# First loads of a fused attention and feed-forward kernel: 2 KB query runs, two heads on a partition, and gate weights loaded by row halves

## The chip, the cores and the metric

One core of a Trainium2 chip. The metric is the device time of one execution in microseconds (us). "us" of a timed run and "span" of its profile are not the same thing: the span leaves out about 2 us at the edges. A "run" of 1 KB or 2 KB is a contiguous stretch of memory that a load reads; it shows in the DMA views as one packet. A run is called slow when it lies over 1.5% above the fastest of its kernel.

## The reference

Linear attention without softmax, an RMS norm per head, then an RMS norm over all heads and a gated feed-forward network:

```python
kv  = einsum("bhsd,bhse->bhde", k, v)            # q, k, v: 8 x 8 x 576 x 64, fp32
out = einsum("bhsd,bhde->bhse", q, kv)
out = out / sqrt(mean(out*out, -1) + 1e-6) * g_norm
x   = out.transpose(0, 2, 1, 3).reshape(8*576, 512)
xn  = x / sqrt(mean(x*x, -1) + 1e-6) * rms_g
y   = (silu(xn @ w_gate) * (xn @ w_val)) @ w_out   # d_ff = 1536
```

## The kernel before: the parts that matter

The work goes batch by batch. PE (the matmul engine) is fed from weights that are loaded as fp32, scaled by `rms_g` and rounded to bf16 on POOL, DVE and ACT (`round_w`), and from queries that are cast to bf16 and transposed on PE. All loads below are issued by SP (`nc.sync`), but for the first value loads and two tiny gain loads by ACT (`nc.scalar`).

Loads of the first batch and of the first weights (`S` = 576, `H` = 8 heads, `NS` = 4 row groups of the weights; cuts are marked):

```python
    q0 = stage().rearrange("p (f h x) -> p f h x", f=2, h=H // 2)

    def load_q0(f, queue):                        # token half f, 256 tokens
        dst = q0[:, f].rearrange("(p g) h x -> p g h x", g=2)
        for g in range(2):                        # 4 tokens of a head are one run: 1 KB
            src = q[0, 4 * g : 4 * g + 4, 256 * f : 256 * f + 256, :].rearrange("h (p t) d -> p h (t d)", t=4)
            queue.dma_start(out=dst[:, g], in_=src)

    for j in (0, 1):
        load_kv(0, "k", nc.sync, slice(j, j + 1))
        load_kv(0, "v", nc.scalar, slice(j, j + 1))
    ...                                           # two loads of gains into gam on nc.scalar
    load_q0(0, nc.sync)
    for j in (2, 3):
        load_kv(0, "k", nc.sync, slice(j, j + 1))
        load_kv(0, "v", nc.sync, slice(j, j + 1))
    load_q0(1, nc.sync)
    load_w("g", (0, 1), False)                    # block 0, then block 1: 1 KB runs
    load_w("v", (0, 1), True)                     # rows 0, 1 of both blocks, then 2, 3: 2 KB runs
```

The order of work on the first weights. `round_w(block, name, row group, engine)` makes one block of 256 columns of one row group ready; `GP` is POOL, `SC` is ACT:

```python
    for s in range(NS):
        round_w(0, "g", s, GP)
    for s in (0, 1):
        round_w(1, "g", s, GP)
    ...
    round_w(1, "g", 2, DVE)
    round_w(1, "g", 3, SC)
    for blk, s in ((0, 0), (0, 1), (1, 0), (1, 1), (0, 2), (1, 2)):
        round_w(blk, "v", s, GP)
    ...                                           # PE: gate products of block 0 in between them
    Z.sums()                                      # the norm's sums of the second token half
    ...
```

After these come the next loads, in this order, and some 20 us later the transposes of the second batch's queries on PE, between parts of the first batch's last product.

```python
    ...                                           # the other gate and value blocks
    load_kv(1, "k", nc.sync)
    load_wo(0, (0,))
    load_kv(1, "v", nc.sync)
    load_wo(0, (2,))                              # second half of a block of the last weights
    load_q(1)                                     # second batch's queries, two loads of 4 heads
    ...
    for c in range(4):
        down_part(c, 0, 2)
    ...                                           # second batch: kv products; casts of its queries
    down_part(0, 2, 4)                            # needs the second half of that block
    turns.q_turn(0, SC)                           # PE transposes; needs both loads of load_q(1)
    down_part(1, 2, 4)
    turns.q_turn(1, DVE)
```

Of the kernel before, what the change touches and what calls it, by code (L numbers as in the profile page):

```python
# [11 lines left out]
BF16 = mybir.dt.bfloat16  # L12
# [8 lines left out]
def kernel(  # L21
# [12 lines left out]
    nc = tc.nc  # L34

    B, H, S, D = q.shape
# [8 lines left out]
    NS = d_model // 128  # L45
# [30 lines left out]
    PE, DVE, SC, GP = nc.tensor, nc.vector, nc.scalar, nc.gpsimd  # L76

    identity = consts.tile([128, 128], BF16, name="identity")
# [20 lines left out]
    def stage(n=2048):  # L99
        return stage_pool.tile([128, NS * C * D], FP32, name="st")[:, 0:n]  # L100

    def cast(engine, dst, src):
        if engine is SC:
            engine.copy(out=dst, in_=src)  # L104
        else:
            engine.tensor_copy(out=dst, in_=src)  # L106
# [7 lines left out]
    def alloc_kv(b, name):  # L114
        raws[b, name] = stage(NS * C * D).rearrange("p (j x) -> p j x", j=NS)
# [51 lines left out]
    def load_w(name, blks, split):  # L167

        widths = [(W_BLOCKS[b][1] - W_BLOCKS[b][0]) * 128 for b in blks]
        j0 = W_BLOCKS[blks[0]][0] * 128  # L170
        view, flat, at = {"g": wg_view, "v": wv_view}[name], stage(), 0
        whole = flat[:, 0 : NS * sum(widths)].rearrange("p (s f) -> p s f", s=NS)
        for b, w in zip(blks, widths):
            if split:
                w_st[name, b] = whole[:, :, at : at + w]
            else:
                w_st[name, b] = flat[:, NS * at : NS * (at + w)].rearrange("p (s f) -> p s f", s=NS)
                nc.sync.dma_start(out=w_st[name, b], in_=view[:, :, j0 + at : j0 + at + w])
            at += w
        if split:  # L180
            for s in (0, 2):
                nc.sync.dma_start(out=whole[:, s : s + 2], in_=view[:, s : s + 2, j0 : j0 + at])
# [282 lines left out]
    class Ffn:  # L465
# [68 lines left out]
        def down_out(self, c, engine=None):  # L534
            if c % 2 == 0:
                self.o_sb = osb_pool.tile([128, 2, d_model], FP32, name="o_sb")
            cast(engine or SC, self.o_sb[:, c % 2, :], self.o_ps[c])
            n = self.n
            if n == B:
                for u in range(2):  # L540
                    r0 = (2 * c + u) * S + MAIN
                    nc.sync.dma_start(
                        out=out[r0 : r0 + TAIL, :], in_=self.o_sb[u * TAIL : (u + 1) * TAIL, c % 2, :]
                    )
            elif c % 2 == 1 and n == 0:
                r0 = 256 * (c // 2)
                rows = out[r0 : r0 + 256, :].rearrange("(p c t) d -> t p c d", c=2, t=2)
                for t in range(2):
                    nc.sync.dma_start(out=rows[t], in_=self.o_sb[64 * t : 64 * t + 64])
            elif c % 2 == 1:  # L550
                rows = out[n * S : n * S + MAIN, :].rearrange("(p t) d -> p t d", t=T)[:, c - 1 : c + 1, :]
                nc.sync.dma_start(out=rows, in_=self.o_sb)
# [32 lines left out]
    b0 = 0  # L585
    for name in ("k", "v"):
        alloc_kv(0, name)
    q0 = stage().rearrange("p (f h x) -> p f h x", f=2, h=H // 2)

    def load_q0(f, queue):  # L590

        dst = q0[:, f].rearrange("(p g) h x -> p g h x", g=2)
        for g in range(2):
            src = q[0, 4 * g : 4 * g + 4, 256 * f : 256 * f + 256, :].rearrange("h (p t) d -> p h (t d)", t=4)
            queue.dma_start(out=dst[:, g], in_=src)

    for j in (0, 1):
        load_kv(0, "k", nc.sync, slice(j, j + 1))
# [4 lines left out]
        out=gam[NS : NS + 1, :].rearrange("o (i d) -> o i d", i=2),  # L603
        in_=g_norm.rearrange("(o d) -> o d", o=1).unsqueeze(1).to_broadcast([1, 2, D]),
    )
    load_q0(0, nc.sync)
    for j in (2, 3):
        load_kv(0, "k", nc.sync, slice(j, j + 1))
        load_kv(0, "v", nc.sync, slice(j, j + 1))
    load_q0(1, nc.sync)  # L610
    load_w("g", (0, 1), False)
    load_w("v", (0, 1), True)

    make_identity(nc, identity)
    make_identity(nc, ident32)
# [11 lines left out]
    def warm(ps, count, w=512):  # L627
        for _ in range(count):
            PE.matmul(ps[:, 0:w], lhsT=warm_sb[:, 0:128], rhs=warm_sb[:, 0:w], start=True, stop=True, skip_group_check=True)  # L629
# [5 lines left out]
    qb0 = bufs[0]["q"]  # L635
    qt0 = qt_pool.tile([128, NS, MAIN], BF16, name="qt")
# [1 line left out]
    A = Cols(0, 0, 256, qt0, sqt0, "A")  # L638
    Z = Cols(0, 256, 512, qt0, sqt0, "Z")

    qb0 = qb0.rearrange("p t h d -> p (t h d)").rearrange("p (f t h d) -> p f t h d", f=2, t=4, h=4)

    def cast_q0(f, hs, engine):
        cast(engine, qb0[:, f, :, hs, :], q0[:, f, hs, :].rearrange("p h (t d) -> p t h d", t=4))

    def turn_q0(f, dummies):
        bank = att_pool.tile([128, 512], FP32, name="att_ps")
        warm(bank, dummies)
        ps = bank.bitcast(BF16).rearrange("p (j t x) -> p j t x", j=2, t=4)
        for j in range(2):  # L650
            for t in range(4):
                PE.matmul(
                    ps[:, j, t, :], lhsT=qb0[:, f, t, 2 * j : 2 * j + 2, :], rhs=identity,
                    is_transpose=True, start=(j == 0 and t == 0), stop=(j == 1 and t == 3),
                )
        return ps.rearrange("p j t (x g) -> p j t x g", g=2)

    def put_q0(f, ps, g, engine):
        dst = qt0[:, 2 * g : 2 * g + 2, 256 * f : 256 * f + 256].rearrange("p j (t x) -> p j t x", t=4)
        cast(engine, dst, ps[:, :, :, :, g])  # L660

    def state0(j, dummies):
        ps = att_pool.tile([128, 512], FP32, name="att_ps")
# [30 lines left out]
            cols.o_products(c, banks[c])  # L694
        return banks

    hs0, hs1 = slice(0, 2), slice(2, 4)

    warm_ps = att_pool.tile([128, 512], FP32, name="att_ps")
    warm(warm_ps, 9)  # L700
# [1 line left out]
    for j in (0, 1):  # L702
# [3 lines left out]
    kv1 = state0(1, 3)  # L706
    put_state0(0, kv0)
    cast_q0(0, hs0, DVE)
    cast_q0(0, hs1, SC)
    put_state0(1, kv1)  # L710
    banksA = [gps_pool.tile([128, MAIN], FP32, name="g_ps"), vps_pool.tile([128, MAIN], FP32, name="v_ps")]
    qps = turn_q0(0, 2)
    cast_kv(0, "k", 2, DVE)
    cast_kv(0, "v", 2, SC)
    put_q0(0, qps, 0, DVE)
    put_q0(0, qps, 1, SC)
    kv2 = state0(2, 3)
    cast_kv(0, "k", 3, DVE)
# [13 lines left out]
        out=gsq, in0=gcol, scalar=1.0 / d_model, in1=gcol, op0=OP.mult, op1=OP.mult  # L732
# [9 lines left out]
    A.sums()  # L742
    oA = rows_of(A)
    cast_q0(1, hs0, SC)
    cast_q0(1, hs1, GP)
    A.head()
    A.root_by_table(lambda: None)
    banksZ = [gps_pool.tile([128, MAIN], FP32, name="g_ps"), vps_pool.tile([128, MAIN], FP32, name="v_ps")]
    qps = turn_q0(1, 2)
    warm(banksZ[0], 2)  # L750
    for g in range(2):
        put_q0(1, qps, g, SC)
# [321 lines left out]
```

## Time and profile before

| what | value |
|---|---|
| time, three runs | 319.03 median (318.98 to 319.62) us |
| time, six runs beside the changed kernel (the three are among them) | 319.4 median, 319.45 mean (318.98 to 319.96) us |
| span of the profile, granted clock | 317.6 us, 0.998 |
| PE busy | 97% of the span |
| start of PE's row of 16 gate and value products (the head's weights are there) | 22.43 us |
| cast of the second half of batch 1's queries | 42.51 us |
| start of batch 1's first attention products on PE | 45.48 us |

The last three are the marks by which I compare profiles.

Third, the timeline at 42 to 44 us. DVE, idle, waits 0.81 us for a load of batch 1's queries (in brackets), casts it, and the eight transposes on PE, which take 0.61 us where nothing holds them, take 0.99.

```profile
42.51 0.63 DVE L106 CAST qb<-st 128x512 bf16<-128x512 f32 x2 [0.81 <-DMA st<-in_q_dram]
42.73 0.99 PE L843 MATMUL g_ps<-identity,qb 128*128 128x128 bf16 x8
43.78 0.38 PE L529 MATMUL o_ps<-wo_sb,h_sb 128*128 128x512 bf16 x1
```

### The profile page before, as it was taken

To read this page: it belongs to the slowest core of one execution; us is meant where nothing else is said; L and a number is where in the kernel's file an instruction comes from. 1 tells how busy PE (TensorE), PEld (TensorE's weight loads), DVE (VectorE), ACT (ScalarE), POOL (GpSimd) and SP (SyncE) were. 2 spreads that over 40 slices of the span, in tenths; PEclk is the share of its full clock that TensorE was granted. 3 is DMA by queue.
4 is the path that set the end of the run, shared out by engine and by line. 5 is a ranking of instruction groups with operands and counts; after the bars stand their busy time and mean duration, and the time that the engine had idled before them with its cause. 6 is when DMAs were issued, how large, how long until landed. Compare 5 with 4: busy or idle time off the path is not lost.

```text
span 317.6 us, 5996 instructions
## 1 busy us (share of the span) xinstructions
PE 308.5 (97%) x2334; PEld 150.3 (47%) x2371; DVE 181.3 (57%) x378; ACT 175.6 (55%) x323; POOL 21.5 (7%) x46
## 2 busy tenths in 40 slices
PE   7899999999999999999999999999999999999995
PEld 3575446444444444444444444444444444444443
DVE  3776768679339922893289327941795079504310
ACT  3577367485667465746683768376745374233321
POOL 1174351100000000000000000000000000000000
PEclk9999999999999999999999999999999999999999
DMA  7999999685369267904790489939002710230014
GB/s 266 358 385 388 375 375 333 145 275 215 90 180 344 86 138 187 369 9 108 189 378 22 98 172 207 354 66 181 22 0 60 140 66 3 57 141 3 0 33 100
DMA packets 60712, 54.95 MB, mean 173 GB/s; under 512 B 36232, under 2 KB 45708, under 8 KB 60684
## 3 DMA queue, kind: packets, MB, share of 16 engines
q1 hardware_dynamic: 60304, 53.92, 56.7%
q10 hardware_dynamic: 380, 0.66, 0.6%
q8 instruction: 18, 0.29, 0.4%
q14 instruction: 10, 0.08, 0.1%
HBM read 37.75 MB, written 9.44 MB: 149 GB/s over the span
## 4 chain that ended last, share of the span: by engine, by line
PE 90%; DMA 5%; SPq 1%; another core or an unknown queue 1%; issue 1%; POOL 1%; DVE 0%; ACT 0%
PE v_ps L477 28%; PE g_ps L477 28%; PE o_ps L529 26%; DMA st<-in_moe_w_val_dram 3%; DMA st<-in_q_dram 2%; PE att_ps L286 2%; PE v_ps L529 1%; PE g_ps L529 1%; DMA out_dram<-o_sb 1%; PE att_ps L326 1%; PE o_ps L494 1%; POOL wv_sb L191 1%; PE o_ps L326 0%; PE att_ps L262 0%
## 5 line engine op out<-in xcount | busy, mean ns | idle before, releaser
L483 DVE TENSOR_TENSOR h_sb<-silu,v_ps 128x512 bf16<-128x512 bf16 x104 | 71.1, 684 | 99.9 <-ACT silu L482 68.1
L477 PE MATMUL v_ps<-xnt,wv_sb 128*128 128x512 bf16 x409 | 106.2, 379 | 0.7
L477 PE MATMUL g_ps<-xnt,wg_sb 128*128 128x512 bf16 x398 | 104.6, 379 | 0.7
L482 ACT ACTIVATE silu<-g_ps 128x512 bf16<-128x512 f32 x104 | 62.1, 597 | 70.1 <-PE g_ps L477 58.4
L529 PE MATMUL o_ps<-wo_sb,h_sb 128*128 128x512 bf16 x386 | 86.8, 379 | 0.4
L477 PEld LDWEIGHTS <-wv_sb 128*128 128x128 bf16 x416 | 40.7, 98 | 49.1
L529 PEld LDWEIGHTS <-h_sb 128*128 128x128 bf16 x420 | 40.6, 98 | 47.6 <-issue 0.4
L477 PEld LDWEIGHTS <-wg_sb 128*128 128x128 bf16 x416 | 39.5, 98 | 46.4
L104 ACT COPY o_sb<-o_ps 128x512 f32<-128x512 f32 (+1 forms) x34 | 19.6, 581 | 40.2 <-PE o_ps L529 36.6
L373 DVE TENSOR_TENSOR xna<-outa,s1y 128x512 bf16<-128x512 bf16 x28 | 17.9, 685 | 0.0
L104 ACT CAST qb<-st 128x512 bf16<-128x512 f32 (+1 forms) x30 | 16.2, 603 | 3.0 <-DMA st<-in_q_dram 3.0
L104 ACT CAST vb<-st 128x576 bf16<-128x576 f32 x25 | 15.7, 673 | 3.4 <-DMA st<-in_v_dram 3.4
L356 DVE TENSOR_REDUCE ssq<-sq 128x16 f32<-128x1024 bf16 x14 | 17.1, 1220 | 0.5
L356 DVE TENSOR_REDUCE ssq<-sqt 128x16 f32<-128x1024 bf16 x14 | 17.1, 1220 | 0.5
L104 ACT CAST kb<-st 128x576 bf16<-128x576 f32 x20 | 12.5, 673 | 0.0
L341 ACT ACTIVATE sq<-att_ps 128x512 bf16<-128x512 f32 x14 | 7.6, 594 | 4.3 <-PE att_ps L326 3.6
L355 DVE TENSOR_TENSOR sq<-sq,gsq 128x512 bf16<-128x512 bf16 x14 | 5.9, 422 | 4.9 <-ACT sq L341 4.9
L629 PE MATMUL att_ps<-kv_all 128*128 128x512 bf16 (+1 forms) x21 | 7.5, 486 | 1.2 <-DVE sel L618 1.2
L106 DVE CAST kb<-st 128x576 bf16<-128x576 f32 x12 | 6.1, 527 | 3.6 <-DMA st<-in_k_dram 3.5
L106 POOL CAST wo_sb<-st 128x512 bf16<-128x512 f32 x12 | 7.3, 635 | 7.4 <-DMA st<-in_moe_w_out_dram 7.4
L341 ACT ACTIVATE sqt<-o_ps 128x512 bf16<-128x512 f32 x14 | 7.6, 597 | 0.0
L347 ACT CAST outa<-o_ps 128x512 bf16<-128x512 f32 x14 | 7.5, 591 | 0.0
(150 smaller groups left out, 181.5 us busy)
## 6 DMA issues: line engine op xcount, KB each, us to landing
st<-in_k_dram SPq DMA_DIRECT2D x7, 1152.0 KB, 10.5
st<-in_v_dram SPq DMA_DIRECT2D x7, 1152.0 KB, 12.6
out_dram<-o_sb SPq DMA_DIRECT2D x14, 512.0 KB, 3.1
st<-in_q_dram SPq DMA_DIRECT2D x6, 1024.0 KB, 7.2
st<-in_moe_w_out_dram SPq DMA_DIRECT2D x6, 512.0 KB, 10.4
st<-in_moe_w_gate_dram SPq DMA_DIRECT2D x4, 512.0 KB, 10.4
st<-in_moe_w_val_dram SPq DMA_DIRECT2D x4, 512.0 KB, 9.8
st<-in_k_dram SPq DMA_DIRECT2D x4, 288.0 KB, 4.0
```

What stands on the lines that cost most here:

```text
L104: engine.copy(out=dst, in_=src)
L106: engine.tensor_copy(out=dst, in_=src)
L286: PE.matmul(self.kv_ps[x][to, a, :], lhsT=kb[rows, 2 * a + x, c, :], rhs=vb[rows, 2 * a + x, c, :], start=(a == 0 and c == 0), stop=(a == ...
L341: SC.activation(out=self.in_place(self.sq[i][:, 0], g), in_=bank, func=ACT.Square)
L347: SC.copy(out=self.in_place(rows, g), in_=bank)
L356: DVE.reduce_sum(out=self.ssq[:, c], in_=sq, axis=AX.X)
L373: DVE.tensor_tensor(out=self.xna[c], in0=self.outa[c], in1=self.alpha[:, c, :].to_broadcast([128, H, D]), op=OP.mult)
L477: PE.matmul(ps, lhsT=wt[:, s, j * 128 : (j + 1) * 128], rhs=x[:, s, :], start=(s == 0), stop=(s == NS - 1),)
L482: SC.activation(out=silu, in_=g_ps, func=ACT.Silu)
L483: DVE.tensor_tensor(out=self.h[:, j, :], in0=silu, in1=v_ps, op=OP.mult)
L529: PE.matmul(self.o_ps[c], lhsT=self.h[:, j, c * 128 : (c + 1) * 128], rhs=wo_sb[:, j, :], start=(j == 0), stop=(j == NF - 1),)
L629: PE.matmul(ps[:, 0:w], lhsT=warm_sb[:, 0:128], rhs=warm_sb[:, 0:w], start=True, stop=True, skip_group_check=True)
```

## The change

The intent: in the stretch of the head where the loads are the bound, half of the bytes go in runs of 1 KB. The queries of the first batch are laid out with 8 tokens of a head in one run (2 KB) and two heads on a partition, and the gate weights are loaded as the value weights already were, by row halves of both blocks. Counts of transposes, casts and copies stay; the output's row order follows the new token order, in 8 issues in place of 4.

```diff
-                rows = out[r0 : r0 + 256, :].rearrange("(p c t) d -> t p c d", c=2, t=2)
-                for t in range(2):
-                    nc.sync.dma_start(out=rows[t], in_=self.o_sb[64 * t : 64 * t + 64])
+                rows = out[r0 : r0 + 256, :].rearrange("(p c t) d -> t p c d", c=2, t=4)
+                for t in range(4):
+                    nc.sync.dma_start(out=rows[t], in_=self.o_sb[32 * t : 32 * t + 32])
@@ load_q0
-        dst = q0[:, f].rearrange("(p g) h x -> p g h x", g=2)
-        for g in range(2):
-            src = q[0, 4 * g : 4 * g + 4, 256 * f : 256 * f + 256, :].rearrange("h (p t) d -> p h (t d)", t=4)
-            queue.dma_start(out=dst[:, g], in_=src)
+        src = q[0, :, 256 * f : 256 * f + 256, :].rearrange("(g h) (p t) d -> h p g (t d)", h=2, t=8)
+        for h in range(2):
+            queue.dma_start(out=q0[:, f, h, :], in_=src[h])
@@ loads
-    load_w("g", (0, 1), False)
-    load_w("v", (0, 1), True)
+    for name in ("g", "v"):
+        load_w(name, (0, 1), True)
@@ turn_q0, put_q0 (cut: the same eight transposes, copies that read every fourth element)
-        for j in range(2):
-            for t in range(4):
-                PE.matmul(ps[:, j, t, :], lhsT=qb0[:, f, t, 2 * j : 2 * j + 2, :], ...)
+        for t in range(8):
+            PE.matmul(ps[:, t, :], lhsT=qb0[:, f, t], ...)
```

More of the change, by code (lines that the diff above doesn't have):

```diff
@@ L587 @@
         alloc_kv(0, name)
-    q0 = stage().rearrange("p (f h x) -> p f h x", f=2, h=H // 2)
+    q0 = stage().rearrange("p (f h x) -> p f h x", f=2, h=2)
     def load_q0(f, queue):
-        dst = q0[:, f].rearrange("(p g) h x -> p g h x", g=2)
-        for g in range(2):
-            src = q[0, 4 * g : 4 * g + 4, 256 * f : 256 * f + 256, :].rearrange("h (p t) d -> p h (t d)", t=4)
-            queue.dma_start(out=dst[:, g], in_=src)
+        src = q[0, :, 256 * f : 256 * f + 256, :].rearrange("(g h) (p t) d -> h p g (t d)", h=2, t=8)
+        for h in range(2):
+            queue.dma_start(out=q0[:, f, h, :], in_=src[h])
     for j in (0, 1):
@@ L639 @@
     Z = Cols(0, 256, 512, qt0, sqt0, "Z")
-    qb0 = qb0.rearrange("p t h d -> p (t h d)").rearrange("p (f t h d) -> p f t h d", f=2, t=4, h=4)
+    qb0 = qb0.rearrange("p t h d -> p (t h d)").rearrange("p (f t h d) -> p f t h d", f=2, t=8, h=2)
     def cast_q0(f, hs, engine):
-        cast(engine, qb0[:, f, :, hs, :], q0[:, f, hs, :].rearrange("p h (t d) -> p t h d", t=4))
+        cast(engine, qb0[:, f, :, hs, :], q0[:, f, hs, :].rearrange("p h (t d) -> p t h d", t=8))
     def turn_q0(f, dummies):
@@ L648, in turn_q0, with put_q0 @@
         warm(bank, dummies)
-        ps = bank.bitcast(BF16).rearrange("p (j t x) -> p j t x", j=2, t=4)
-        for j in range(2):
-            for t in range(4):
-                PE.matmul(
-                    ps[:, j, t, :], lhsT=qb0[:, f, t, 2 * j : 2 * j + 2, :], rhs=identity,
-                    is_transpose=True, start=(j == 0 and t == 0), stop=(j == 1 and t == 3),
-                )
-        return ps.rearrange("p j t (x g) -> p j t x g", g=2)
-    def put_q0(f, ps, g, engine):
-        dst = qt0[:, 2 * g : 2 * g + 2, 256 * f : 256 * f + 256].rearrange("p j (t x) -> p j t x", t=4)
-        cast(engine, dst, ps[:, :, :, :, g])
+        ps = bank.bitcast(BF16).rearrange("p (t x) -> p t x", t=8)
+        for t in range(8):
+            PE.matmul(
+                ps[:, t, :], lhsT=qb0[:, f, t], rhs=identity, is_transpose=True, start=(t == 0), stop=(t == 7),
+            )
+        return ps.rearrange("p t (x g) -> p g t x", g=NS)
+    def put_q0(f, ps, i, engine):
+        js = slice(2 * i, 2 * i + 2)
+        dst = qt0[:, js, 256 * f : 256 * f + 256].rearrange("p j (t x) -> p j t x", t=8)
+        cast(engine, dst, ps[:, js])
     def state0(j, dummies):
@@ L695, in rows_of @@
         return banks
-    hs0, hs1 = slice(0, 2), slice(2, 4)
+    hs0, hs1 = slice(0, 1), slice(1, 2)
     warm_ps = att_pool.tile([128, 512], FP32, name="att_ps")
```

## The prediction

> **What bounds the kernel now.** I first read the page: one core, clock 0.998, span 317.6 us, PE busy 97%. Then its table of slices and the chain of work that ended last: from about 22 us on PE is the chain, with 90% of the span, and only the head and the tail of the run are anything else. So a change of the first loads can be worth only what it takes off the head.
>
> ```profile
> PE 308.5 (97%) x2334; PEld 150.3 (47%) x2371; DVE 181.3 (57%) x378; ACT 175.6 (55%) x323; POOL 21.5 (7%) x46
> PE 90%; DMA 5%; SPq 1%; another core or an unknown queue 1%; issue 1%; POOL 1%; DVE 0%; ACT 0%
> ```
>
> Next the chain cut to the first 60 us (start, length, what). The reader is to see that one load, the first half of the value weights (issued at 9.52, landed at 18.54), ends the head: POOL scales four of its blocks, PE multiplies by them, and the chain goes over to PE. Three more lines, from the timeline of POOL, show that POOL was idle until the load came and that it does six weight blocks in 2.79 or 2.76 us, 0.465 us each.
>
> ```profile
> 1.64 5.34 DMA st<-in_q_dram
> 9.52 9.03 DMA st<-in_moe_w_val_dram
> 18.63 1.86 POOL wv_sb L191 x4
> 20.53 0.50 PE v_ps L503 x3
> 22.43 1.91 PE o_ps L494 x16
> ```
> ```profile
> 13.62 0.61 POOL L106 CAST qb<-st 128x512 bf16<-128x512 f32 x1 [12.04 <-DMA st<-in_q_dram]
> 15.10 2.79 POOL L191 TENSOR_SCALAR wg_sb<-st,rowscale 128x256 bf16<-128x256 f32 x6 [0.86 <-DMA st<-in_moe_w_gate_dram]
> 18.63 2.76 POOL L191 TENSOR_SCALAR wv_sb<-st,rowscale 128x256 bf16<-128x256 f32 x6 [0.74 <-DMA st<-in_moe_w_val_dram]
> ```
>
> Why does it land at 18.54? Between 5 and 25 us the table of windows gives a DMA share above 1.0: the sixteen DMA engines are never idle, the issues run 5 to 9 us ahead of their data. So the landing is bytes over rate. The DMA view cut into pieces of 2 us gives the rate by packet size; below are the pieces 10 to 12, 12 to 14 and 18 to 20 us. In the first two nearly every packet is under 2 KB (the second half of the queries and the two gate loads, all in 1 KB runs): 319 and 334 GB/s. In the third nearly all are 2 KB or more: 384 GB/s, with the engines just as busy.
>
> ```profile
> DMA packets 655, 0.64 MB, mean 319 GB/s; under 512 B 36, under 2 KB 652, under 8 KB 655
> DMA packets 670, 0.67 MB, mean 334 GB/s; under 512 B 17, under 2 KB 670, under 8 KB 670
> DMA packets 403, 0.77 MB, mean 384 GB/s; under 512 B 28, under 2 KB 28, under 8 KB 403
> ```
>
> **What the Trainium skill says.** (1) "DMA: Bandwidth & Descriptors", section "Why small descriptors are slow (HBM only)": a fixed cost of about 3 cycles a packet beside 32 B a cycle, and 32 B of metadata. By that a 1 KB run takes 35 cycles and a 2 KB run 67, so two of 1 KB would cost 4% more than one of 2 KB. The trace agrees in direction, not in size: 384 over 326 is 18%. I use the trace. (2) "Perfetto Trace Analysis", section "DMA Optimizations", says that DMAs under 2 KB have a significant overhead of their own; that agrees with the lines above. (3) "DMA: Bandwidth & Descriptors", section "Why a DMA increments its semaphore by 16 and not by 1": a load counts as landed only when every engine that carries a share is through. The trace agrees: counted by bytes, the last 1 KB packets are gone at about 14.8 us (230 of the 14 to 16 us piece), so at 384 GB/s the 0.52 MB after them would end at 16.2; they landed at 18.54. The slowest engine runs some 2 us behind the mean; I take this lag to stay. (4) "Advanced Engine Details and Errata", section "2x-2p Requirements": a copy within SBUF gets two elements a cycle if the outer sizes of both sides are even. The query cast on DVE now takes 426 ns for 512 elements, which fits; afterwards its outer size is 8, still even, so I expect no change.
>
> **Part by part.** *Queries.* Before: 4 loads of 256 KB, each 256 runs of 1 KB. After: 4 loads of 256 KB, each 128 runs of 2 KB. *Gate.* Before: 2 loads of 512 KB, each 512 runs of 1 KB. After: 2 of 512 KB, each 256 runs of 2 KB. So 2.10 MB (half queries, half gate) change from 326 to 384 GB/s: 6.43 us become 5.46, a saving of 0.97 us in front of the value weights. By the landing of the second half of the queries it is 0.48, by the second gate load 0.97. Issue gets shorter too (about 0.7 us for a query load against 0.34 to 0.43 for a key load of 128 runs), but issue waits for nothing that is short: no gain.
>
> *What the split by rows gives back.* Before, the first gate load carried all four row groups of block 0, landed at about 15.0 and let POOL do block 0 and two groups of block 1 in one row, 15.10 to 17.89. Afterwards the first load carries groups 0 and 1 of both blocks, the second groups 2 and 3. The order on POOL is unchanged, so its third gate block waits for the second load. That landed before 16.94 (ACT started on it then without a wait); I take 16.8, hence 15.9 to 16.1 afterwards. POOL then needs four blocks: 16.0 + 4 x 0.465 = 17.9. The value weights land at 18.54 - 0.97 = 17.6. So POOL, not the load, starts the value blocks, at about 17.9 instead of 18.63: **the 0.97 us become 0.75**. The same wait holds up the first gate products: block 0 is complete at 16.0 + 0.93 = 16.93, against 15.10 + 4 x 0.465 = 16.96 before: even.
>
> *The norm of the second token half.* Its sums are behind those gate products in PE's order, so they stay at 17.3; its two scalings end at 19.9 and 20.5 on DVE as before. PE wanted them at 20.87 and 21.53, afterwards at about 20.1 and 20.8. The slack shrinks from 1.0 to some 0.3 us, but holds.
>
> *First token half.* Its end hangs on the last key and value loads (cast at 10.74, state copied at 11.76). These lie behind only the first half of the queries and move forward by 0.2 us. The transposes (8 on 128 columns each half), the casts and the copies out of PSUM keep their number and size; the copies read every fourth bf16 in place of every second. At 692 ns on DVE for 512 elements, against 425 for the contiguous ones, they are already at one element a cycle, so no change: 0.
>
> *Semaphores.* The listing of the changed kernel shows a shift: the third key load no longer waits for the first one (it did until 4.46 us), but the tiny load of the gain vector on ACT now does, and ACT's first value cast stands behind it: about 5.1 instead of 4.63. Its product stands before one that waits for 6.17 + 0.67, so I put this at 0.
>
> *Output.* The first batch's rows go out in 8 issues of 128 KB in place of 4 of 256 KB. They took 3.09 us for 4 at 59.8 us; 4 more push the next batch's loads back by about 3 us. These are wanted well over 10 us later, and no DMA wait shows between 60 and 130 us: 0.
>
> **Sum.** 0.75 us off the head; PE, which from 22.4 us never waits for a load, keeps the rest of its length: 319.03 - 0.75 = 318.3 us.
>
> **Rivals.** *A: the gain is lost to POOL's new wait.* If the second gate load lands at 16.6 rather than 16.0, block 0 is ready at 17.5, the norm sums slip by 0.5 and POOL gets to the value blocks at 18.5: the gain is 0.1 to 0.2, time 318.9. For it speaks that POOL has no spare time there and that no trace line gives that landing exactly; against it, that the bytes ahead of it shrink most. *B: the full saving of the loads, or more.* If the slow engine gains more than the mean (the last gate load and the first value load together took it 3.5 us, the second value load only 1.4), the second gate load could land at 15.5 and all later steps with it, also the norm; then 1.2 us, time 317.8. *C: run length doesn't matter.* If the low rate at 10 to 14 us comes from the row pitch of these loads in memory, not from 1 KB packets, nothing moves: 319.0. Against: queries and weights have quite different pitches and the same rate. *D: a later limit.* PE starts 0.75 us sooner into weights that come by DMA; if these don't come sooner, it stalls. The queue moves forward by 0.97, more than PE: unlikely.
>
> **Range and chances.** B's end is 317.8, A's and C's 318.9 to 319.0; with 0.1 to 0.2 of run scatter (before: 318.98 to 319.62) I say 317.6 to 319.0. Two per cent are 6.4 us; the head as a whole has little more than that to give, and nothing added is of that size: faster 0.01, same 0.98, slower 0.01.
>
> **What would show it.** Right: 10 to 14 us now at 375 GB/s or more with few packets under 2 KB; the second query half cast at about 13.1 (was 13.57); POOL's gate blocks broken in two, a wait after the second; value blocks on POOL at about 17.9 with no or hardly any DMA wait; PE's L494 run of 16 at about 21.7 (was 22.43). Wrong: the rate stays near 330 (C); POOL's value blocks start after 18.3 (A); PE waits for vector work of the second norm at 20 to 21 us (the slack gone); or new waits on loads between 22 and 60 us (D). A time under 317.6 or over 319.0 would mean that I missed a term.

## More of the kernel before

The chain of waits, the POOL rows and the rates at 10 to 20 us stand in the prediction. Three things that it does not show are needed later. First, the DMA view over 2 to 18 us, the time in which the loads in question pass: the packets, the bytes moved, the mean rate.

```profile
DMA packets 3952, 5.73 MB, mean 358 GB/s; under 512 B 261, under 2 KB 2313, under 8 KB 3951
```

Second, the timeline of SP: when it issues the second half of the queries, the gate and the value weights (start, length, line, what).

```profile
7.00 1.27 SPq L595 DMA_DIRECT2D st<-in_q_dram  x2
8.32 1.15 SPq L178 DMA_DIRECT2D st<-in_moe_w_gate_dram  x2
```

## The result and the profile after

The changed kernel took 319.21 us (median of six runs, 318.76 to 320.16), the kernel before, on the same chip between them, 319.4 (318.98 to 319.96). The ratio is 0.9995 [0.9976, 1.0014]: the same. Here and below a ratio is the mean time of one kernel's fast runs over that of the other's of the same rounds, so not quite the ratio of the medians; the brackets are its 95% interval. The prediction of 318.3, range 317.6 to 319.0, was wrong: the time lies above the range.

The span went from 317.6 to 316.8 us, just what was predicted, and this is the trap: one profile of each kernel would have confirmed the prediction. It was luck in part: the profiled run of the changed kernel was the fastest of its six (318.76 us), that of the kernel before took 319.61. The chain of waits after, cut to the first 60 us:

```profile
8.61 0.59 SPq L182
9.25 6.98 DMA st<-in_moe_w_gate_dram
16.31 0.95 POOL wg_sb L191 x2
17.30 0.45 PE g_ps L494 x5
...
22.04 1.91 PE o_ps L494 x16
```

The load on the chain is no longer the first half of the value weights but the second half of the gate: it lands at 9.25 + 6.98 = 16.23, POOL scales two blocks of it, and PE's gate products follow. The timeline of POOL shows the same: the gate row is broken in two, and the value blocks start with no wait.

```profile
15.07 0.94 POOL L191 TENSOR_SCALAR wg_sb<-st,rowscale 128x256 bf16<-128x256 f32 x2 [1.86 <-DMA st<-in_moe_w_gate_dram]
16.31 1.88 POOL L191 TENSOR_SCALAR wg_sb<-st,rowscale 128x256 bf16<-128x256 f32 x4 [0.31 <-DMA st<-in_moe_w_gate_dram]
18.16 2.75 POOL L191 TENSOR_SCALAR wv_sb<-st,rowscale 128x256 bf16<-128x256 f32 x6
```

On PE, the first gate products now wait for POOL. The norm's sums of the second token half, behind them in order, start at 17.59 (17.29 before).

```profile
17.30 0.45 PE L494 MATMUL g_ps<-xnt,wg_sb 128*128 128x128 bf16 x5 [0.23 <-POOL wg_sb L191]
17.59 0.20 PE L419 MATMUL att_ps<-epsrow,ones 128*128 128x8 bf16 x2
```

The DMA view of the pieces 10 to 12, 12 to 14 and then of 2 to 18 us. The short packets are gone (267 under 2 KB in place of 2313: the 2048 runs of the edit), but in the first piece the rate is 336 GB/s where 375 or more was foretold, and over the whole stretch no more than 1% more has moved (5.80 MB for 5.73).

```profile
DMA packets 361, 0.67 MB, mean 336 GB/s; under 512 B 34, under 2 KB 34, under 8 KB 361
DMA packets 377, 0.73 MB, mean 367 GB/s; under 512 B 19, under 2 KB 19, under 8 KB 377
...
DMA packets 2964, 5.80 MB, mean 362 GB/s; under 512 B 263, under 2 KB 267, under 8 KB 2963
```

The table of windows says why that may be: the DMA engines' busy share was 1.03 in both pieces before, and is 0.96 and 0.99 now. There was not always a packet to move. The rows of 10 to 12 us, before and after (busy us of PE, PEld, DVE, ACT and POOL, then clock, DMA share, GB/s):

```profile
10.00:12.00 2.00, 2.00 (x42) 1.14 (x41) 1.77 (x8) 1.26 (x3) 0.00 (x0) 1.00 1.03 319
10.00:12.00 2.00, 1.73 (x42) 1.13 (x42) 1.60 (x7) 1.45 (x4) 0.00 (x0) 1.00 0.96 336
```

SP's waits up to 16 us for loads of keys, values and queries (what was waited for, us in all, times, longest); before they were 2.0 us for keys, in two waits, and 0.2 for queries:

```profile
SPq L119 <- DMA st<-in_v_dram: 0.9, 1, 0.9
SPq L119 <- DMA st<-in_k_dram: 0.9, 1, 0.9
SPq L594 <- DMA st<-in_q_dram: 0.8, 1, 0.8
```

At these places SP does not issue a load until an earlier one has landed. By the listing of the program, that is because its loads are given a handful of semaphores in turn; the traces show the waits. The second half of the queries and the gate went out 0.4 and 0.3 us later than before (in the second pair of profiles, below, 0.14 and 0.06):

```profile
7.37 1.20 SPq L594 DMA_DIRECT2D st<-in_q_dram  x2
8.61 1.10 SPq L182 DMA_DIRECT2D st<-in_moe_w_gate_dram  x2
```

At 42 us the cast of batch 1's second query half now starts at 41.48 and PE's transposes, at 42.35, are not held up:

```profile
41.48 0.63 DVE L106 CAST qb<-st 128x512 bf16<-128x512 f32 x2 [0.24 <-DMA st<-in_q_dram]
42.35 0.61 PE L842 MATMUL g_ps<-identity,qb 128*128 128x128 bf16 x8
```

So of the 0.77 us between 45.48 and 44.71 (batch 1's attention products), 0.39 had been gained by 22 us, and 0.38 more at 42 us, at a wait that the prediction did not have.

### The profile page after: what moved, and what is told of

Its sections match the earlier page's. It is cut to its first block, busy times and chain, and to the rows that moved or that the text cites. A ratio compares the mean times of both kernels' runs of the same rounds, so it can differ in the third digit from the quotient of the medians.

```text
span 316.8 us, 5999 instructions
## 1 busy us (share of the span) xinstructions
PE 307.5 (97%) x2334; PEld 150.1 (47%) x2371; DVE 181.3 (57%) x378; ACT 175.5 (55%) x323; POOL 21.6 (7%) x46
## 4 chain that ended last, share of the span: by engine, by line
PE 91%; DMA 5%; SPq 1%; another core or an unknown queue 1%; issue 1%; POOL 0%; DVE 0%; ACT 0%
PE v_ps L477 29%; PE g_ps L477 28%; PE o_ps L529 26%; DMA st<-in_moe_w_gate_dram 2%; DMA st<-in_q_dram 2%; PE att_ps L286 2%; PE g_ps L494 1%; PE v_ps L529 1%; PE g_ps L529 1%; DMA out_dram<-o_sb 1%; PE att_ps L326 1%; PE o_ps L494 1%; PE o_ps L326 0%; PE att_ps L262 0%
## 5 line engine op out<-in xcount | busy, mean ns | idle before, releaser
L373 DVE TENSOR_TENSOR xna<-outa,s1y 128x512 bf16<-128x512 bf16 x28 | 17.9, 685 | 0.0
L347 ACT CAST outa<-att_ps 128x512 bf16<-128x512 f32 x14 | 7.5, 591 | 0.0
```

Source lines behind the costliest of these rows:

```text
L347: SC.copy(out=self.in_place(rows, g), in_=bank)
L373: DVE.tensor_tensor(out=self.xna[c], in0=self.outa[c], in1=self.alpha[:, c, :].to_broadcast([128, H, D]), op=OP.mult)
```

## The experiments

Four questions, from the theories as they stood. **Run length:** packets of 1 KB are slow, and the gain is what their share says. **Queue (Q):** in the changed kernel the DMA engines run dry between landings, as the loads are issued too late. **Late limit:** PE is held by batch 1's queries at 42 us, so a gain before that is not a gain of the whole. **Scatter:** the head differs from run to run by as much as the gain, and one profile of each says little. The expectations are quoted. All kernels gave correct results.

The table has every run: times as median (lowest to highest) of the fast runs, the ratio to the kernel before in the same rounds, then the marks of its profile in us.

| run | us | ratio to before | row of 16 at | batch 1 query cast | batch 1 attention | span |
|---|---|---|---|---|---|---|
| before | 319.4 (318.98 to 319.96) | | 22.43 | 42.51 | 45.48 | 317.6 |
| after | 319.21 (318.76 to 320.16) | 0.9995 [0.9976, 1.0014] | 22.04 | 41.48 | 44.71 | 316.8 |
| before_again | 319.22 (318.84 to 320.35) | 0.9992 [0.9973, 1.0011] | 21.54 | 42.01 | 44.98 | 317.1 |
| after_again | 319.19 (318.91 to 320.81) | 0.9994 [0.9974, 1.0014] | 21.37 | 41.71 | 44.68 | 316.9 |
| q_only | 319.15 (318.84 to 320.21) | 0.999 [0.9973, 1.0007] | 23.13 | 43.16 | 46.12 | 318.2 |
| gate_only | 319.27 (318.59 to 320.36) | 0.999 [0.9972, 1.0009] | 22.25 | 42.31 | 45.28 | 317.4 |
| wts_1k | 320.79 (319.48 to 321.45) | 1.0029 [1.0002, 1.0056] | 24.09 | 43.68 | 46.76 | 318.8 |
| before_pool | 319.38 (319.02 to 319.93) | 0.9994 [0.998, 1.0009] | 22.28 | 42.27 | 45.24 | 317.3 |
| after_pool | 319.23 (318.7 to 320.85) | 0.9996 [0.9975, 1.0018] | 21.17 | 41.24 | 44.21 | 316.6 |
| combo | 318.82 (318.68 to 319.07) | 0.9977 [0.9962, 0.9992] | 21.34 | 41.30 | 44.26 | 316.6 |
| extra_load | 319.57 (318.95 to 321.23) | 0.9994 [0.9972, 1.0017] | 21.48 | 42.87 | 45.84 | 317.9 |
| swap_q | 318.68 (318.62 to 319.04) | 0.9963 [0.9947, 0.9979] | 21.39 | 39.97* | 44.30 | 316.7 |
| swap_before | 319.62 (318.86 to 320.19) | 0.9998 [0.9978, 1.0018] | 22.02 | 41.44 | 45.65 | 317.8 |
| swap_after | 319.24 (318.5 to 320.19) | 0.999 [0.9969, 1.0012] | 22.97 | 41.54* | 45.87 | 318.1 |

(* All four casts of DVE follow one another without a wait there, and this is the start of the first.) Read first the two last columns: the span less the start of batch 1's attention is 272.0 to 272.4 us in every run. Whatever differs between two profiles here is made in the first 46 us.

Then compare the columns before it. In nine of the eleven profiles with the loads in their first order (all but the three swaps) batch 1's attention starts 2.96 or 2.97 us after the query cast, wherever the cast lies. The other two are `after` (3.23) and `wts_1k` (3.08), in which PE's transposes are not held up; in these two 22.67 us lie between the row of 16 and batch 1's attention. What a profile has over 22.67 is how long PE is held at 42 us: 0.38 and 0.77 in the two profiles of the kernel before, 0 and 0.64 in the two of the changed one. So in most profiles a load that lands at 41 to 43 us, and not the first weights, sets the end of the head.

The expectations speak of marks M1, M2 and M3. I use batch 1's attention in place of M3: in the first two profiles the record of one of the two products at M3 is missing, so 43.78 and 43.01 are about 0.2 us late.

### The same two kernels again, and each part alone

Edits: `after_again` and `before_again` are copies. The parts:

```diff
 q_only: after, with
-    for name in ("g", "v"):
-        load_w(name, (0, 1), True)
+    load_w("g", (0, 1), False)
+    load_w("v", (0, 1), True)
 gate_only: before, with the reverse
```

> The changed kernel once more, as it stands. Three marks are read from its profile: M1, the start of POOL's row of four wg_sb blocks of the second weight group (22.70 before, 21.72 after: how far ahead the load stream is); M2, the start of PE's L494 run of 16 into o_ps (22.43 before, 22.04 after); M3, the start of the first o_ps product after the first query turn of batch 1 (43.78 before, 43.01 after). Theory 1 (the loads really gain about 1 us and PE keeps 0.4 of it at M2 and another 0.4 at M3; the six timed runs only hide it in their scatter): M1 21.5 to 21.9, M2 21.8 to 22.2, M3 42.8 to 43.2, ratio of the times 0.9965 to 0.9990. Theory 2 (the one profile of after was a lucky draw and the change is worth 0.2 us or less): marks scattered by half a us or more around those of before, ratio 0.999 to 1.001.

> The kernel before, against itself, for the floor of both measures. Every theory: ratio 1.000 with an interval of some 0.001 to 0.002 on either side, M1 22.7, M2 22.4, M3 43.8, each within 0.2. If a mark moves by more than 0.3 without any change, the marks cannot carry theory 1.

> The query part alone (2 KB runs, eight output issues), with the two gate loads as before, in 1 KB runs and by block. Theory 1, run length sets the rate: half the bytes changed, so half of the stream's lead: M1 22.1 to 22.3. The first gate load again completes block 0, so POOL scales six gate blocks in one row from about 14.6 to 15.1, and the value weights bind again at 20.0 to 20.2: M2 21.9 to 22.1, M3 43.2 to 43.5. Theory 3, the split by row groups costs what the gate's longer runs bring: M2 here is not later than that of the whole change (22.04). Theory 2: all marks as before.

> The gate part alone (two loads by row groups, 2 KB runs), with the queries as before. Theory 1: M1 22.1 to 22.3. Second gate load at about 16.6, so block 0 is complete on POOL only at about 17.5, the norm sums slip by 0.5: Theory 3 (POOL's wait gives the gain back) says M2 22.2 to 22.6, so nothing or next to nothing at M2, and M3 at 43.3 to 43.6 by the stream alone. If instead M2 is 22.0 or earlier, the split costs nothing and the query part is what gives less than reckoned.

Measured: all four took the time of the kernel before, within intervals of about 0.2% (0.6 us), and `before_again`, which is the kernel before, came out as low against it as any. In the profiles the unchanged kernel moved by more than the change did: its row of 16 products at 21.54, 0.89 us before that of its first profile (22.43), against 0.39 between the first pair. Between the second pair the change gives 21.54 − 21.37 = 0.17. The DMA view over 2 to 18 us, `before_again` and `after_again`:

```profile
DMA packets 4011, 5.85 MB, mean 365 GB/s; under 512 B 263, under 2 KB 2315, under 8 KB 4010
```
```profile
DMA packets 3018, 5.90 MB, mean 368 GB/s; under 512 B 270, under 2 KB 274, under 8 KB 3017
```

The expectation for `before_again` had the row of 16 within 0.2 of 22.4: it missed. Again a lead of 1%, 0.05 MB, which at 365 GB/s is 0.14 us; in the first pair it was 0.07 MB, 0.19 us. And again the slow piece at 10 to 12 us is there without a short packet to blame, in `after_again` even at 301 GB/s with the engines 0.96 busy:

```profile
DMA packets 323, 0.60 MB, mean 301 GB/s; under 512 B 29, under 2 KB 29, under 8 KB 323
```

That the low rate comes from run length alone is thereby refuted. `q_only` shows the scatter at its plainest: by 18 us it had moved 5.87 MB, more than either profile of the kernel before, and yet its second gate load was the latest of these profiles (17.9 us; POOL waits 1.11 us for it), and everything after it is late (row of 16 at 23.13, expected 21.9 to 22.1). Its timed runs are not, but for the profiled one, which was the slowest of its six (320.21). One doubt stays: `wts_1k` below has the same query and gate loads, and there the second gate load is as late (POOL starts on it at 18.26). Two profiles do not tell chance from a property of this combination.

```profile
17.99 1.09 POOL L191 TENSOR_SCALAR wg_sb<-st,rowscale 128x256 bf16<-128x256 f32 x2 [1.11 <-DMA st<-in_moe_w_gate_dram]
```

What follows: the landing of a load differs by about 1 us between runs of the same kernel, not in step with the bytes moved, and single profiles can't size an effect below that. Over the 12 runs of the changed kernel and the 23 of the unchanged in these two sessions, the means differ by 0.1 us, with ± 0.4 us as the 95% interval of that difference. So the predicted 0.75 is excluded, and 0 is not. The parts alone can't be told from the whole.

### Why the rate stays low: the queue runs dry

By the same listing the two tiny gain loads on ACT (2 KB and 0.5 KB) hold two of the semaphores that SP's loads take in turn. Moved to POOL's queue they hold none of them, and SP waits for older loads. The same in both kernels:

```diff
-    nc.scalar.dma_start(out=gam[0:NS, :], ...)
-    nc.scalar.dma_start(out=gam[NS : NS + 1, :]..., ...)
+    nc.gpsimd.dma_start(out=gam[0:NS, :], ...)
+    nc.gpsimd.dma_start(out=gam[NS : NS + 1, :]..., ...)
```

> The changed kernel with the two tiny loads (norm gains) issued by POOL instead of ACT. They leave the eight semaphores that the loads share in turn, so that each later load of the head waits for an older load than before: the second query half is issued once the second key and value loads are in (about 6 us) instead of the first query loads (6.9 to 8.0), the gates at 7.4 to 8 instead of 8.1 to 9.2. Theory Q (the trough at 10 to 14 us of the changed kernel, where the DMA share falls to 0.95 to 1.00, is the queue run dry: loads are issued too late, so faster runs buy idle engines): DMA share 1.03 or more in each 2 us from 8 to 16, rate above 360 at 10 to 14, value weights and M1 0.5 us or more ahead of after (M1 21.2 or less), ratio 0.996 to 0.999. Theory S (the memory is slow in that stretch whatever is issued): share up, rate still under 340 at 10 to 12, M1 within 0.2 of after, ratio 0.998 to 1.001.

> The same edit on the kernel before. Its engines were already busy throughout (share 1.03 and more), so earlier issue buys nothing by theory Q: M1 21.8 to 22.7, M2 21.5 to 22.4 as in its two profiles, rate 319 to 345 at 10 to 14 us; ratio 0.999 to 1.001. Set beside after_pool it is the change's worth with the issue out of the way: by Q and R together after_pool is ahead of it by 0.5 to 1.0 us, by S by 0.2 or less.

Measured: SP now issues the second query half of the changed kernel at 5.85 us (7.37) and the gate at 7.09 (8.61), as its timeline shows,

```profile
5.85 1.20 SPq L594 DMA_DIRECT2D st<-in_q_dram  x2
7.09 1.10 SPq L182 DMA_DIRECT2D st<-in_moe_w_gate_dram  x2
```

and the slow piece is gone. The DMA view at 10 to 12 and 12 to 14 us, first `after_pool` (2 KB runs), then `before_pool` (1 KB):

```profile
DMA packets 407, 0.77 MB, mean 383 GB/s; under 512 B 33, under 2 KB 33, under 8 KB 407
DMA packets 414, 0.78 MB, mean 392 GB/s; under 512 B 31, under 2 KB 31, under 8 KB 414
```
```profile
DMA packets 734, 0.73 MB, mean 367 GB/s; under 512 B 43, under 2 KB 714, under 8 KB 734
DMA packets 704, 0.70 MB, mean 352 GB/s; under 512 B 16, under 2 KB 704, under 8 KB 704
```

The busy share is 1.05 in both pieces of `after_pool` and 1.08 and 1.10 in `before_pool`: I take the queue to be full in both, so that this pair measures run length by itself. It is 387.5 against 359.5 GB/s, 8%. For the 2.10 MB of the change that is 5.84 − 5.42 = 0.42 us, not 0.97. It is one pair of profiles. Other full pieces of 1 KB runs show 368 GB/s (`before_again`, 12 to 14 us, share 1.09) and 372 (`wts_1k`, 14 to 16 us, 1.13), which makes it 4 to 8%; and by 18 us `after_pool` is 6.05 − 5.78 = 0.27 MB ahead of `before_pool`, 0.7 us. So run length with a full queue is worth some 0.4 to 0.7 us. Queue theory and run-length theory thus both had a part of the low 319 and 334 GB/s of the kernel before. For the queue speak all profiles: at 10 to 12 us the ten without this edit show 261 to 354 GB/s, the four with it 367 to 394. My expectation for `before_pool`, 319 to 345 GB/s at 10 to 14 us since a share of 1.03 was taken for a full queue, failed. But by 18 us its 5.78 MB lie between the two profiles without the edit (5.73 and 5.85).

The Trainium skill, "DMA: Bandwidth & Descriptors", section "Issuing engines are not separate DMA queues", says that starting DMAs from several engines saves only the sequencer's time for starting them. Here the move brought the gate's issue forward by 1.0 to 1.5 us (8.61 and 8.09 in the two profiles of the changed kernel, 7.09 now) and, by 18 us, 6.05 MB in place of 5.80 or 5.90, though what was moved took almost no bytes: the gain lies in what the other loads no longer wait for.

In time, however, neither kernel gained (0.9996, expected 0.996 to 0.999, and 0.9994), although the profile of `after_pool` has its row of 16 products at 21.17, 1.11 us before `before_pool`. One profile, once more, of a fast draw: that run took 318.7 us, the lowest of the six of `after_pool`, whose highest was 320.85.

### More of the weights in 1 KB runs

```diff
     for name in ("g", "v"):
-        load_w(name, (0, 1), True)
+        load_w(name, (0, 1), False)
```

> The changed kernel, but with its first gate loads and its first value loads by blocks of 256 columns, all four in 1 KB runs: 2.1 MB in short runs, as many bytes as the change made long. The queue is full at 14 to 18 us, when the value weights come, and their pitch in memory is that of the value weights in the kernel before, so the rate there tells run length from everything else. Theory R (run length sets the rate, as predicted): 325 to 350 GB/s at 14 to 18 us where the other kernels have 365 to 407, and the stream's mark M1 (POOL's row of four wg_sb blocks, 21.6 and 21.7 in the two profiles of after) at 22.5 to 22.7. Theory S (it is not run length: the 10 to 12 us stretch is slow in every profile, 301 to 336 GB/s, with 2 KB packets as well): 375 to 390 GB/s at 14 to 18 us, M1 at 21.5 to 22.0.

Measured: 320.79 us, ratio 1.0029, slower by 0.9 us or so (the interval, 1.0002 to 1.0056, only just leaves out 1). Against the changed kernel this puts back the gate's 1 MB into 1 KB runs and adds the value weights' 1 MB. By the 8% above that is worth about 0.4 us of transfer. The test set beforehand, the rate at 14 to 18 us, fell between the theories: 372 and 349 GB/s, where R had 325 to 350 and S 375 to 390; M1 came at 23.92, later than either said. For the rest of the time there are two candidates that this run does not part: its 10 to 12 us piece, at 261 GB/s and a busy share of 0.94, is the slowest of all profiles, and with the loads by blocks the row groups land in another order than POOL's. So this run fits the direction of the change, but does not show it apart from these, nor size it.

### Where the head ends: 256 KB more ahead of batch 1's queries

A load that nobody reads, in front of `load_q(1)`:

```diff
+    spare = consts.tile([128, 512], FP32, name="spare")
+    nc.sync.dma_start(out=spare, in_=wg_view[:, 0, 0:512])
     load_q(1)
```

> The changed kernel with one more load of 256 KB that nobody reads, put into the stream ahead of batch 1's queries, far behind the value weights. It tells what sets the end of the head: M2 (PE's start into the second token half, 21.4 and 22.0 in the two profiles of after) must not feel it. Theory L (the head ends where batch 1's second query half lands, at about 42 us; PE waits for it whatever it won at 22): that landing and M3 move by 262144 B over 387 GB/s = 0.68 us, to 43.4 to 43.8 from 42.8 and 43.0, the span with them, ratio of the times 1.001 to 1.003. Theory P (the prediction: PE waits for no load after 22 us): M3 and the span as in after, ratio 0.998 to 1.001.

Measured: the row of 16 products stays early, at 21.48. At 42 us the timeline reads:

```profile
42.87 0.63 DVE L106 CAST qb<-st 128x512 bf16<-128x512 f32 x2 [0.88 <-DMA st<-in_q_dram]
43.36 0.73 PE L844 MATMUL g_ps<-identity,qb 128*128 128x128 bf16 x6 [1.00 <-DVE qb L106]
```

PE waits a full 1.00 us for DVE, DVE for the load, and batch 1's attention starts at 45.84, 1.1 us later than in either profile of the changed kernel. This shows the late limit in the profile: the cast is 1.16 us later than in `after_again` (0.68 was expected), and batch 1's attention is 1.16 later too, whatever was won at 22 us. PE is held 1.69 us by the measure under the table. In time the load shows little: 319.57, in the same rounds as the kernel before at 319.9 (ratio 0.9994, where this theory asked for 1.001 to 1.003). So what the limit costs in time is not shown.

### Taking that limit away

`combo` is `after_pool` with one gate block moved from POOL, which was the next in line, to DVE:

```diff
-    for s in range(NS):
+    for s in range(3):
         round_w(0, "g", s, GP)
@@ in the loop over x_turn(A, i, ...)
+        if i == 0:
+            round_w(0, "g", 3, DVE)
```

`swap_q` is `combo` with batch 1's queries ahead of the half block of output weights, in the loads and on PE:

```diff
-    load_wo(0, (2,))
     load_q(1)
+    load_wo(0, (2,))
@@
-    down_part(0, 2, 4)
     turns.q_turn(0, SC)
-    down_part(1, 2, 4)
     turns.q_turn(1, DVE)
-    for c in range(2, 4):
+    for c in range(4):
         down_part(c, 2, 4)
```

> after_pool, and the fourth row group of the first gate block is scaled by DVE between its two copies of the first token half, so that POOL has only one block of it left behind the second gate load. If the gain is given back at POOL's wait for the second gate load (theory 3): PE starts the rest of its first gate products 0.3 us sooner after that load's landing (0.65 instead of 1.0 us), POOL comes to the value blocks 0.47 us sooner unless these then have to be waited for, and M2 is 0.2 to 0.4 us ahead of that of after_pool. If not, M2 as after_pool. Best guess for the ratio 0.995 to 0.999.

> combo, with batch 1's queries loaded before the second half of the first output weight block, and PE turning both query pairs ahead of the four products that need that half. The queries lie 0.5 MB earlier in the stream, so they land 1.35 us sooner, at about 39.9 us. Theory L: PE's wait at the query turn (0.4 us in combo, its turn of eight taking 0.87 to 0.99 instead of 0.61) goes, and the time falls by 0.2 to 0.4 us below combo: ratio to before 0.9955 to 0.998, span 316.2 to 316.4. Theory P: as combo, span 316.6, unless the half that is now later makes PE wait in its place (it lands at about 41.3 and POOL needs 1.2 us for it; PE wants it at about 42.4).

Measured: `combo` 318.82 us, ratio 0.9977 [0.9962, 0.9992]; `swap_q` 318.68 us, ratio 0.9963 [0.9947, 0.9979]. These are the only two versions whose interval lies wholly below the kernel before, and their runs hold within 0.4 us where the others spread over 0.9 to 2.3 us. In the profile of `swap_q` the query wait is gone and a shorter one, for the output weights, has come in its place:

```profile
41.26 0.62 PE L844 MATMUL g_ps<-identity,qb 128*128 128x128 bf16 x8
...
42.70 0.81 PE L529 MATMUL o_ps<-wo_sb,h_sb 128*128 128x512 bf16 x3 [0.16 <-POOL wo_sb L106]
```

Its start of batch 1's attention, 44.30, is no earlier than `combo`'s 44.26. Nor is `combo`'s earlier than `after_pool`'s 44.21: by the profiles the moved gain loads made the head short, and the gate block on DVE and the swap added nothing to the fastest case. What they added in time must then be in the other runs, which have no profile: it looks like steadiness, and that is argued, not shown. In the rounds that they share, `combo`'s mean lies 0.63 us under `after_pool`'s, with ± 0.7 as its 95% interval; theory 3, which had `combo`'s row of 16 0.2 to 0.4 us ahead of `after_pool`'s, failed (21.34 and 21.17). The gate block on DVE was not run by itself. `combo` and `swap_q` were timed in different sessions, so which of them is the faster is open. Against the changed kernel's means (319.28 and 319.43) `swap_q`'s, 318.73, is lower by 0.6 us, again across sessions.

### The swap alone

The swap of `swap_q` alone, on the kernel before and on the kernel after.

> The kernel before, with only the new order of loads and products from swap_q (batch 1's queries ahead of the second half of the first output weight block). Theory L: PE's wait at the query turn, 0.4 us in both profiles of before, goes; the turns of eight run back to back (0.62 us each), ratio 0.997 to 0.999. The early limit (value weights at 18 us, M2 at 21.5 to 22.4) is untouched, so run scatter stays near 1 us.

> The changed kernel with the same new order and nothing else: beside swap_before this is the worth of the change with the later wait out of its way. The stream's lead of the change was 1% of bytes by 18 us (362 and 368 against 358 and 365 GB/s), so 0.15 us; with the predicted full rate gain it would be 0.75. I expect 0.1 to 0.4 us under swap_before, ratio to before 0.996 to 0.9985, under the noise against swap_before.

Measured: nothing in either (0.9998, expected 0.997 to 0.999, and 0.999, expected 0.996 to 0.9985). The transposes no longer wait, but the load that went behind the queries is now the late one:

```profile
43.49 0.38 PE L529 MATMUL o_ps<-wo_sb,h_sb 128*128 128x512 bf16 x1 [0.39 <-POOL wo_sb L106]
```

My expectation for `swap_before`, that the wait would go, failed: 0.39 us for queries became 0.39 us (and 0.18 more) for output weights. I read this so: at this place PE is held by the stream of loads as such, not by one load of it, and only a stream that runs ahead helps. `swap_after`'s profile happened on a run of 320.19 us, with its head late from the value weights on, and its marks can't be set against the others. Up to 40 us the two are the kernels before and after once more: by 18 us they had moved 5.62 and 5.86 MB, a lead of 0.24 MB or 0.65 us, and still the changed one's row of 16 was 0.95 us later (22.97 against 22.02).

## Why the prediction was wrong

The predicted 318.28 and the measured mean of 319.28 (median 319.21) are 1.0 us apart. Of this 0.42 is the starting point: 319.03 was the median of three runs, the mean of the six beside the changed kernel is 319.45, and later medians were 319.72 to 319.9. The other 0.58 is the gain, 0.17 in that comparison where 0.75 was predicted. Step by step:

- **"2.10 MB ... change from 326 to 384 GB/s ... a saving of 0.97 us": this step failed.** A DMA share of 1.03 was read as "never idle", and the rate of the 1 KB pieces put down to run length as a whole; with earlier issue the same runs moved at 359.5 GB/s with shares of 1.08 and 1.10. Run length is worth 387.5 against 359.5 GB/s (full queue, `after_pool` and `before_pool`), 0.42 us; the 4% that the prediction estimated and set aside was nearer to this than its 18%. Also, a quarter of the 2.10 MB, the first half of the queries, had no low rate to lose: at 4 to 6 and 6 to 8 us, with their 1 KB packets among the others, the profile before shows 380 and 364 GB/s, that after 385 and 370. And even the 0.42 did not come in whole: in the changed kernel SP's issues waited for landings, the DMA engines went dry at 10 to 12 us, and the lead of the stream by 18 us was 0.14 to 0.19 us in the two pairs of profiles (0.65 in the pair of the swaps).
- **"Issue waits for nothing that is short": failed too**, and has a part in the above, as the runs with the gain loads moved show. I took the issues to be 5 to 9 us ahead of their data and so never short. But an issue that waits for an earlier landing moves with it. I had seen the shift of the waits in the listing ("Semaphores") and counted only its effect on ACT's cast (predicted 5.1, measured 5.11), not on the queue.
- **"I take this lag to stay": not so.** The lag of the last engine behind the mean differs by about 1 us between runs of one kernel. The range allowed 0.1 to 0.2 us of scatter, from three runs; single runs of the kernel before spread from 318.69 to 320.30 on one chip (to 320.65 over all).
- **"The 0.97 us become 0.75", by POOL's new wait: right in kind.** The gate row broke in two; value blocks began at 18.16, without a DMA wait (predicted 17.9), as the second gate load landed at 16.23 (predicted 15.9 to 16.1). Rival A had this landing at 16.6 and the norm's sums 0.5 us late; they came 0.3 us late, with PE waiting 0.23 us for POOL. What took place lies between my sum and A. Rival C's number, 319.0, is nearest to the measured time, but not for C's reason: with the queue full the longer runs were faster (387.5 against 359.5 GB/s).
- **"PE, which from 22.4 us never waits for a load": failed.** PE waits at 42 us for batch 1's queries, in three of the four profiles of the two kernels, and is held there by 0.38 to 0.77 us. The profile before showed it already: the eight transposes at 0.99 us in place of 0.61. `extra_load` shows the single wait grow to 1.00. Rival D was dismissed because the queue moves forward more than PE; in the second pair it did not (0.14 us, and PE's row of 16 by 0.17).
- **The remaining terms held, but one.** The first token half was to come 0.2 us sooner; its last value cast came 0.3 later (11.04 for 10.74), and in the second pair at the same time (10.50). Transposes, casts and the copies that read every fourth element kept their times (0.43 for a cast on DVE, 0.69 and 0.58 for the copies); the 8 output issues cost PE nothing; the second norm's slack lasted.
- **The profile agreed with a wrong number.** The first pair of profiles gave 0.77 us. It was half made at 22 us and half at 42 us, the second pair gave 0.30 (44.98 to 44.68), and `before_pool` with `after_pool` 1.03. The profiled runs of the changed kernel were the fastest or second fastest of their six (318.76, 318.98, 318.70), so these pairs flatter the change.

Shown: the failing of the rate step, the dry queue, the wait at 42 us in the profiles. Sized only roughly, from one pair of profiles: run length. Open: how much of the lost gain went to each of these in time; whether the change is worth 0 or some tenths; and what makes a load's last engine late in one run and not in the next.

## What to carry to other kernels

A low DMA rate in a stretch of short packets has two possible causes, the packets and the supply of issues; look at the busy share, then at what each issue waits for, before giving all of it to the packets. A share just above 1 does not settle it: here 1.03 went with 319 GB/s, and 1.08 with 367, for the same runs. Before a gain below 1 us is predicted from one profile, profile the same kernel twice: what differs between the two is the floor of what can be read. And when a head is shortened, look for the next place at which the same stream of loads is waited for, for there the gain is asked for again.

## What the Trainium skill lacked or had wrong

- "DMA: Bandwidth & Descriptors", "Why small descriptors are slow (HBM only)": an estimate from its 3 cycles a packet beside 32 B a cycle makes 2 KB runs 4% better than 1 KB. With the queue full one pair of profiles shows 387.5 against 359.5 GB/s, 8%; other pieces of 1 KB runs, at 368 and 372, make it 4 to 5%. So the page is not shown to be wrong; the 18% of the first profile was.
- "DMA: Bandwidth & Descriptors", "Issuing engines are not separate DMA queues": it counts only sequencer time as saved by another issuing engine. Two loads of 2.5 KB together, moved to another engine, brought the issue of later loads forward by 1.0 to 1.5 us, as these then waited for older loads.
- "Perfetto Trace Analysis", "DMA Optimizations": it names overhead of small DMAs, and no sign by which to tell it from a queue that ran dry. Here the busy share helped only in part: 0.96 at 301 and 336 GB/s without short packets, 1.08 and 1.10 at 367 and 352 GB/s with them, but 1.03 at 319 GB/s, where both causes were at work.
- No page says how far the landing of one load scatters between runs: the same kernel before had its row of products at 22.43 and at 21.54 us, and timed runs on one chip from 318.69 to 320.30.
